# Linear attention and two gated layers on one Trainium2 core: a planner with other step lengths, a decode that moves, a q product in one piece

## The chip, the cores and the metric

The kernel runs on one core of one Trainium2 chip. The number is the device time in microseconds of one execution, the median of three; a profiled execution of the same program gives the trace. Five engines run side by side, each in its own order: TensorE (PE, matmuls, with PEld for its weight loads), VectorE (DVE), ScalarE (ACT), GpSimd (POOL), and SyncE (SP), whose queue issues the transfers (DMA).

## The reference

```python
kv  = einsum('bhsd,bhse->bhde', k, v)            # 8 batches, 8 heads, 576 tokens, 64 columns
out = einsum('bhsd,bhde->bhse', q, kv)
x   = out / sqrt(mean(out*out, -1) + 1e-6) * g_norm     # then 4608 tokens x 512
x   = (sigmoid(x @ w_gate) * (x @ w_val)) @ w_out       # 512 -> 1536 -> 512
h   = x @ w_in                                          # 512 -> 2048
y   = where(h > 0, h, exp(min(h, 0)) - 1) @ w_out2      # 2048 -> 512
```

## The kernel before

The 4608 tokens are cut in 12 blocks of 384, and two blocks make a group, six groups in all. Each fp32 factor is split in a high and a low part, so that a product is three passes over TensorE (`matmul3`, lines 384 to 386; 714 to 716 in the second layer's output).

**First layer.** For each group: attention of the next group's blocks, `in1` (the two input products and their gate), `out1` (the output product). Group 0 computes `in1` plainly. Groups 1 to 5 use a Strassen-like form (`quad`): seven products of six matmuls each instead of eight, four PSUM banks, and five additions on DVE (`plus`, line 538) that read a bank and free it. TensorE's next use of a bank waits for that addition. A group has 12 quads in `in1`, 60 additions. **Second layer.** All groups pass through `in2` (eight quads, 40 additions, and an ELU of two ACT steps and one DVE step, line 653) and `out2`, in which each product needs a split of its stationary factor: `split` (high part on ACT, line 605, low part on DVE, line 607) into one of three buffers J.

**Attention** of a block: k'v of each batch (lines 410 and 412), its copy to `kvb` (414), two q products (442) that each fill two PSUM banks for two pairs of heads, squares on ACT (449), sums on DVE (450), 13 small operations on 128x24 numbers (lines 458 to 465) that form the reciprocal root, four products with it on DVE (477), four transposes (487). The q product takes the two heads of a pair as two matmuls on 64 rows each.

**Decode.** The weights come as raw 64-bit words. `decode` makes fp32 words of them (273, 275, 277, 281), splits them (294, 296) into a buffer S and stores them; `sums` adds the Strassen sums (POOL 321 to 324, ACT 326, DVE 329). The second layer's 16 decodes (eight of `w_in`, "I", eight of `w_out2`, "O") are placed in `out1` of groups 1 to 4, four in each. The S buffers, five of them, also take the weights that are streamed for the products.

**Order.** Nothing is ordered by hand but TensorE's own list. The class `Plan` simulates all engines with a length for each step, a delay for each hand-over and a due time, and writes the instructions of each engine in the order that comes out. The chip then runs each engine's list in that order. DVE, between a wait and the next, does what the list says, late or not.

Of the kernel before, what the change touches and what calls it, by code (L numbers as in the profile page):

```python
# [21 lines left out]
P = 128  # L22
# [15 lines left out]
T_ACT, T_DVE, T_POOL = 0.53, 0.57, 1.15  # L38
# [21 lines left out]
class Plan:  # L60


    LAT = {"PE": 0.25, "DVE": 0.1, "ACT": 0.1, "POOL": 0.12, "SP": 3.5}
# [54 lines left out]
    def round(self):  # L118
# [32 lines left out]

        def begin(t, at):
# [7 lines left out]
            push(at + t.dur, "end", t)  # L160
# [4 lines left out]
        while events:  # L165
            at = events[0][0]
            while events and events[0][0] <= at + 1e-9:
# [6 lines left out]
                elif what == "free":  # L174
                    free[t.cls].append(t.slot)
                    used[t.kind] -= 1
                else:
                    idle[t.eng] = True
                    for b in t.bufs:
# [27 lines left out]
def tile_kernel(ctx: ExitStack, tc: tile.TileContext, kv, kvtail, qt, g2, w1, w2, out):  # L207
# [17 lines left out]
    kvb = [fixed([P, NP, D], F32, f"kvb{i}") for i in range(2)]  # L225
# [17 lines left out]
    plan.caps.update({"h": 32, "tmp": 11, "xf": 8, "ev": 8, "q": 4, "dec": 4, "dec2": 2, "wh": 2, "wp": 2})  # L243
# [19 lines left out]
    def decode(layer, fp, after=None):  # L263
# [3 lines left out]
        wh, wp = plan.buf("wk", "wh"), plan.buf("wk", "wp")  # L267
        word = []
        for n, f in enumerate(order):
# [3 lines left out]
            a = add("ACT", 0.65, lambda raw=raw, n=n: nc.scalar.activation(  # L273
                wh.slot[:, n, :], raw.slot[:, :, 1].bitcast(F32), AF.Copy, scale=2.0 ** -112), [ld], [raw, wh])
            b = add("ACT", 0.65, lambda raw=raw, n=n: nc.scalar.activation(
                wp.slot[:, n, :].bitcast(I32), raw.slot[:, :, 0].bitcast(U32), AF.Copy, scale=0.93 * 2.0 ** -29), [ld], [raw, wp])
            c = add("DVE", 0.8, lambda raw=raw, n=n: nc.vector.scalar_tensor_tensor(
# [3 lines left out]
        w = add("DVE", 1.3, lambda: nc.vector.scalar_tensor_tensor(  # L281
            wh.slot.bitcast(I32), wh.slot.bitcast(I32), 3, wp.slot.bitcast(I32),
            op0=ALU.logical_shift_left, op1=ALU.bitwise_or), word, [wh, wp])
        sa = plan.buf("S", "dec" if layer in "gvo" else "dec2")
        if layer == "O":
            x_hi, x_lo = (lambda: sa.slot[:, :, 0, :].rearrange("q (h n) c -> q h n c", n=2)), (lambda: sa.slot[:, :, 1, :].rearrange("q (h n) c -> q h n c", n=2))
            src_w = lambda: wh.slot.rearrange("q n (h c) -> q h n c", h=2)
        elif layer == "o":
# [5 lines left out]
        h = add("ACT", 1.05, lambda: nc.scalar.activation(x_hi(), src_w(), AF.Copy), [w, last_hi[0]], [wh, sa])  # L294
        last_hi[0] = h
        l = add("DVE", 1.3, lambda: nc.vector.tensor_tensor(x_lo(), src_w(), x_hi().bitcast(F32), op=ALU.subtract), [h], [wh, sa])  # L296
# [5 lines left out]
        if layer == "O":  # L302
            written[layer, fp] = [dma(P * 8192, lambda: nc.sync.dma_start(out=wo2[:, 0:4, fp], in_=sa.slot.bitcast(F32)), [h, l], [sa])]
            return sa, [h, l]
        d = (ws2 if layer == "I" else ws1["gv".index(layer)])[fp]
        st_a = dma(P * 6144, lambda: nc.sync.dma_start(out=d[:, 0:3], in_=sa.slot[:, 1:4].bitcast(F32)), [h, l], [sa])
        written[layer, fp] = [st_a]
        if layer == "I":
            written[layer, fp].append(sums(layer, fp, wh, w)[2])
        else:  # L310
            written["f", layer, fp] = [dma(P * 4096, lambda: nc.sync.dma_start(out=wf1["gv".index(layer)][fp], in_=wh.slot), [w], [wh])]
        return sa, [h, l]

    def sums(layer, fp, wh, w):


        d = wo2[:, 1:, fp] if layer == "O" else (ws2 if layer == "I" else ws1["gv".index(layer)])[fp]
        sf, sb_ = plan.buf("wk", "wp"), plan.buf("S", "dec2" if layer in "IO" else "st")
        A = lambda i: wh.slot[:, i // 2, i % 2 * 256:i % 2 * 256 + 256]
        T = lambda i: sf.slot[:, i // 2, i % 2 * 256:i % 2 * 256 + 256]  # L320
        s1 = add("POOL", 0.8, lambda: nc.gpsimd.tensor_tensor(T(0), A(0), A(1), op=ALU.add), [w], [wh, sf])
        s3 = add("POOL", 0.8, lambda: nc.gpsimd.tensor_tensor(T(2), A(2), A(0), op=ALU.subtract), [w], [wh, sf])
# [4 lines left out]
        if layer in "gv":  # L327
            h2.early = 12.0
# [548 lines left out]
```

## Time and profile before

| | |
|---|---|
| median of three runs | 1703.45 us (1702.94 to 1705.19) |
| profiled execution | 1705.86 us, span 1704.1 us |
| PE busy | 1670.7 us, 98% of the span |
| DVE, ACT, POOL busy | 1126.9, 810.6, 347.1 us |

The span is from the first to the last instruction. TensorE's records overlap, since matmuls are pipelined, so that its busy share says little about its pace; the idle stretches between its records, and what ended them, say where it waited. Group 1's `in1` starts near 205 us, and the second layer near 1000 us.

### The profile page before, as it was taken

The page shows a single profiled execution, that of the slowest core. Times are in us where ns is not written, and L with a number is a line of the kernel's source. Part 1 is how long each engine was busy: PE and PEld are TensorE (multiplying, and loading weights), DVE is VectorE, ACT ScalarE, POOL GpSimd, SP SyncE. Part 2 cuts the span into 40 slices and gives each one's busy share as a digit, 9 for nine tenths or more (in the row PEclk, how much of TensorE's full clock was granted, in tenths as well). Part 3 has the DMA queues.
Part 4 walks back from the last instruction along what each step waited for, and adds up shares of the span by engine and source line. Part 5 has one row for each costly group of instructions (what it writes and reads, how often), then busy time and mean ns, then how long its engine had stood idle before and what let it go on. Part 6 is the DMA issues. An engine that isn't in the chain of part 4 may idle for free.

```text
span 1704.1 us, 29327 instructions
## 1 busy us (share of the span) xinstructions
PE 1670.7 (98%) x11079; PEld 1627.6 (96%) x11079; DVE 1126.9 (66%) x2052; ACT 810.6 (48%) x1631; POOL 347.1 (20%) x326
## 2 busy tenths in 40 slices
PE   8899999999999999999999999999999999999998
PEld 6899989999899999999999998899999999999998
DVE  5768466844674385459344577768778678678675
ACT  4556324532352253236322465456566566456554
POOL 0001344502240150115022000041040140230330
PEclk9999999999999999999999999999999999999999
DMA  8988888797778787777877499888878778778774
GB/s 307 329 309 304 313 292 296 280 342 280 271 287 292 252 328 287 249 269 277 282 250 285 152 327 364 296 306 299 263 264 298 247 281 288 244 281 296 245 275 161
DMA packets 117310, 480.07 MB, mean 282 GB/s; under 512 B 11440, under 2 KB 37552, under 8 KB 87984
## 3 DMA queue, kind: packets, MB, share of 16 engines
q1 hardware_dynamic: 117168, 478.20, 78.6%
q8 instruction: 87, 1.43, 0.3%
q14 instruction: 55, 0.45, 0.1%
HBM read 393.22 MB, written 84.93 MB: 281 GB/s over the span
## 4 chain that ended last, share of the span: by engine, by line
PE 89%; DVE 7%; issue 2%; DMA 1%; ACT 0%; SPq 0%; DVEq 0%; ACTq 0%
PE psi L384 20%; PE psi L385 19%; PE psi L386 19%; PE psi L716 4%; PE psi L715 4%; PE psi L714 4%; PE psa L385 3%; PE psa L386 3%; PE psa L384 3%; PE psa L442 2%; PE psa L716 2%; PE psa L715 2%; PE psa L714 2%; DVE v L538 1%; PE psa L410 1%
## 5 line engine op out<-in xcount | busy, mean ns | idle before, releaser
L538 DVE TENSOR_TENSOR v<-v,psi 128x384 f32<-128x384 f32 x540 | 297.8, 551 | 278.3 <-PE psi L386 265.6
L384 PE MATMUL psi<-x,S 128*128 128x384 f32 x1056 | 361.0, 342 | 6.7 <-DVE v L538 6.4
L386 PE MATMUL psi<-x,S 128*128 128x384 f32 x1056 | 355.6, 337 | 4.1 <-DVE S L296 4.1
L385 PE MATMUL psi<-x,S 128*128 128x384 f32 x1056 | 355.2, 336 | 0.9 <-DVE x L495 0.9
L607 DVE TENSOR_TENSOR J<-v,J 128x384 fp32r<-128x384 f32 x336 | 200.5, 605 | 120.9 <-ACT J L605 118.3
L605 ACT ACTIVATE J<-v 128x384 fp32r<-128x384 f32 x336 | 175.8, 524 | 217.5 <-PE psa L386 70.9
L384 PE MATMUL psi<-xt,S 128*128 128x384 f32 x648 | 220.7, 341 | 0.2
L386 PE MATMUL psi<-xt,S 128*128 128x384 f32 x648 | 217.5, 336 | 0.0
L385 PE MATMUL psi<-xt,S 128*128 128x384 f32 x648 | 217.2, 335 | 0.0
L384 PEld LDWEIGHTS psi<-x,S 128*128 128x128 f32 x1056 | 199.6, 189 | 10.7 <-DVE v L538 8.2
L386 PEld LDWEIGHTS psi<-x,S 128*128 128x128 f32 x1056 | 199.8, 189 | 4.5 <-DVE S L296 4.5
L385 PEld LDWEIGHTS psi<-x,S 128*128 128x128 f32 x1056 | 199.8, 189 | 1.8 <-DVE x L495 1.4
L574 POOL TENSOR_TENSOR v<-v,v 128x384 f32<-128x384 f32 x90 | 100.4, 1124 | 430.5 <-DVE v L538 358.3
L716 PE MATMUL psi<-S,J 128*128 128x256 f32 x560 | 159.1, 284 | 2.1 <-DVE J L607 2.1
L714 PE MATMUL psi<-S,J 128*128 128x256 f32 x560 | 158.5, 283 | 0.0
L715 PE MATMUL psi<-S,J 128*128 128x256 f32 x560 | 158.5, 283 | 0.0
L384 PEld LDWEIGHTS psi<-xt,S 128*128 128x128 f32 x648 | 122.3, 189 | 2.0 <-DVE v L538 0.8
L651 ACT ACTIVATE v<-v 128x384 f32<-128x384 f32 x144 | 75.2, 523 | 101.3 <-DVE v L538 101.2
L385 PEld LDWEIGHTS psi<-xt,S 128*128 128x128 f32 x648 | 122.2, 189 | 0.0
L386 PEld LDWEIGHTS psi<-xt,S 128*128 128x128 f32 x648 | 122.1, 188 | 0.0
L542 ACT ACTIVATE v<-psi 128x384 f32<-128x384 f32 x108 | 53.1, 491 | 120.9 <-PE psi L386 119.6
L716 PEld LDWEIGHTS psi<-S,J 128*128 128x128 f32 x560 | 107.4, 192 | 3.1 <-DVE J L607 3.1
(146 smaller groups left out, 3407.0 us busy)
## 6 DMA issues: line engine op xcount, KB each, us to landing
S<-wsO SPq DMA_DIRECT2D x78, 1024.0 KB, 6.3
S<-wsI SPq DMA_DIRECT2D x48, 1024.0 KB, 5.2
S<-wso SPq DMA_DIRECT2D x36, 1024.0 KB, 6.9
S<-wsI SPq DMA_DIRECT2D x48, 768.0 KB, 6.4
raw<-w SPq DMA_DIRECT2D x68, 512.0 KB, 6.4
S<-wsg SPq DMA_DIRECT2D x24, 1024.0 KB, 5.4
S<-wsv SPq DMA_DIRECT2D x24, 1024.0 KB, 5.1
S<-wsg SPq DMA_DIRECT2D x30, 768.0 KB, 6.3
```

The lines of the kernel that those rows point to most:

```text
L384: nc.tensor.matmul(acc, wh, xh, start=first, stop=False, skip_group_check=more)
L385: nc.tensor.matmul(acc, wh, xl, start=False, stop=False, skip_group_check=more)
L386: nc.tensor.matmul(acc, wl, xh, start=False, stop=last, skip_group_check=more)
L538: return add("DVE", T_DVE, lambda: nc.vector.tensor_tensor(dst.slot, a.slot, bank[k].slot[:, :BLK], op=ALU.add), after, [dst, a, bank[k]])
L542: s1 = add("ACT", T_ACT, lambda: nc.scalar.activation(t1.slot, bank["a"].slot[:, :BLK], AF.Copy), [p1], [t1, bank["a"]])
L574: t = add("POOL", T_POOL, lambda r=r, b=b: nc.gpsimd.tensor_tensor(r.slot, r.slot, b.slot, op=ALU.mult), [d, s], [r, b])
L605: hi = add("ACT", T_ACT, lambda: nc.scalar.activation(j.slot[:, 0, :], f.slot, AF.Copy), [d], [j, f])
L607: lo = add("DVE", 0.5, lambda: nc.vector.tensor_tensor(j.slot[:, 1, :], f.slot, j.slot[:, 0, :].bitcast(F32), op=ALU.subtract), [hi], [j, f])
L651: a1 = add("ACT", T_ACT, lambda e=e, b=b: nc.scalar.activation(e.slot, ps_or_v(b), AF.Relu, scale=-1.0), [d], [e, b])
L714: nc.tensor.matmul(acc, x[0], w[:, 0], start=st, stop=False, skip_group_check=True)
L715: nc.tensor.matmul(acc, x[0], w[:, 1], start=False, stop=False, skip_group_check=True)
L716: nc.tensor.matmul(acc, x[1], w[:, 0], start=False, stop=last and f == n - 1, skip_group_check=True)
```

## The change

It has three parts. The planner gets other lengths for its steps, and a rule that lengthens a DVE and a POOL step that run at one time without PSUM. The second layer's decode works in place in the word buffers (`wk`) instead of S, stores high and low parts apart, and its 16 instances are spread over groups 1 to 5 (3, 3, 3, 3, 4). The q product takes a pair of heads as one matmul of 128 rows and 128 columns, with the pair's two k'v matrices on the diagonal of a zeroed 128x128 block of `kvb`; each PSUM bank then holds one pair, and a transpose waits for one normalising product instead of two. In the profile of the changed kernel 538 becomes 577, 607 becomes 646, 653 becomes 692, 518 becomes 557, 477 becomes 516, 442 becomes 481, 329 becomes 370.

```diff
-T_ACT, T_DVE, T_POOL = 0.53, 0.57, 1.15
+T_ACT, T_DVE, T_POOL = 0.43, 0.48, 1.0
...
-    LAT = {"PE": 0.25, "DVE": 0.1, "ACT": 0.1, "POOL": 0.12, "SP": 3.5}
+    LAT = {"PE": 0.25, "DVE": 0.13, "ACT": 0.14, "POOL": 0.14, "SP": 3.5}
...
-            end = max(t.started + t.dur for t in order)
+            end = max(t.started + t.dur for t in order if t.eng == "PE")
...
-            push(at + t.dur, "end", t)
+            stop[t] = at + t.dur
+            if t.eng in port and not any(b.cls.startswith("ps") for b in t.bufs):
+                o = port["POOL" if t.eng == "DVE" else "DVE"]
+                if o is not None and stop[o] > at:
+                    d, p = (t, o) if t.eng == "DVE" else (o, t)
+                    both = min(2 * (stop[d] - at), stop[p] - at)
+                    stop[d] += both / 2
+                    stop[p] += 0.3 * both
+                port[t.eng] = t
+            push(stop[t], "end", t)
...
-    kvb = [fixed([P, NP, D], F32, f"kvb{i}") for i in range(2)]
+    kvb = [fixed([P, NP, P], F32, f"kvb{i}") for i in range(2)]
...
-    plan.caps.update({"h": 32, "tmp": 11, "xf": 8, "ev": 8, "q": 4, "dec": 4, "dec2": 2, "wh": 2, "wp": 2})
+    plan.caps.update({"h": 32, "tmp": 11, "xf": 8, "ev": 8, "q": 4, "dec": 4, "wh": 2, "wp": 2, "wh2": 2, "wp2": 1, "sf": 1})
...
+        k = "2" if layer in "IO" else ""
+        wh, wp = plan.buf("wk", "wh" + k), plan.buf("wk", "wp" + k)
         word = []
         for n, f in enumerate(order):
...
+            a = add("ACT", 0.57, lambda raw=raw, n=n: nc.scalar.activation(
...
+        if layer in "IO":
+            d = ws2[fp] if layer == "I" else wo2[:, :, fp]
+            if layer == "I":
+                sf = plan.buf("wk", "sf")
+                A = lambda i: wh.slot[:, i // 2, i % 2 * 256:i % 2 * 256 + 256]
+                T = lambda i: sf.slot[:, i // 2, i % 2 * 256:i % 2 * 256 + 256]
+                s1 = add("POOL", 0.72, lambda: nc.gpsimd.tensor_tensor(T(0), A(0), A(1), op=ALU.add), [w], [wh, sf])
+                s3 = add("POOL", 0.72, lambda: nc.gpsimd.tensor_tensor(T(2), A(2), A(0), op=ALU.subtract), [w], [wh, sf])
+                s2 = add("POOL", 0.72, lambda: nc.gpsimd.tensor_tensor(T(1), T(0), A(2), op=ALU.subtract), [s1], [wh, sf])
+                s4 = add("POOL", 0.72, lambda: nc.gpsimd.tensor_tensor(T(3), A(3), T(1), op=ALU.subtract), [s2], [wh, sf])
+
+            def part(src, after, n0, n1):
+                out = []
+                h = add("ACT", 0.96, lambda: nc.scalar.activation(wp.slot.bitcast(F32R), src.slot, AF.Copy), after, [src, wp])
+                l = add("DVE", 1.14, lambda: nc.vector.tensor_tensor(src.slot.bitcast(F32R), src.slot, wp.slot, op=ALU.subtract), [h], [src, wp])
+                if layer == "I":
+                    view = lambda b: b.slot.rearrange("q f (k n) -> q (f k) n", k=2)[:, 4 - (n1 - n0):]
+                    to = lambda t: d[:, n0:n1, t]
+                else:
+                    view = lambda b: b.slot.rearrange("q n (h c) -> q h n c", h=2)
+                    to = lambda t: d[:, 0:4, t].rearrange("q (h n) c -> q h n c", n=2)
+                for t, b, x in ((0, wp, h), (1, src, l)):
+                    if layer == "I":
+                        out.append(dma(P * 1024 * (n1 - n0), lambda t=t, b=b: nc.sync.dma_start(out=to(t), in_=view(b)), [x], [b]))
+                    else:
+                        for k in range(2):
+                            out.append(dma(P * 2048, lambda t=t, b=b, k=k: nc.sync.dma_start(out=to(t)[:, k], in_=view(b)[:, k]), [x], [b]))
+                return out, l
+
+            st, l = part(wh, [w] + ([s3, s4] if layer == "I" else []), *((0, 3) if layer == "I" else (0, 4)))
+            written[layer, fp] = st
+            if layer == "I":
+                written[layer, fp] = st + part(sf, st[:1] + [l, s3, s4], 3, 7)[0]
+            return
...
-        if layer == "O":
-            written[layer, fp] = [dma(P * 8192, lambda: nc.sync.dma_start(out=wo2[:, 0:4, fp], in_=sa.slot.bitcast(F32)), [h, l], [sa])]
-            return sa, [h, l]
...
-                            for h in range(2):
-                                r, n = slice(h * D, h * D + D), (k * TPB + i) * D
-                                nc.tensor.matmul(o[h].slot[lo - t0:hi - t0, n:n + D], qs[k].slot[r, lo - j * BLK:hi - j * BLK],
-                                                 kvb[b % 2][r, 2 * pp + k, :], start=True, stop=True)
-            m = add("PE", 1.1, mm, lds + sum((kvdone[b, p] for b in bs for p in (2 * pp, 2 * pp + 1)), []), qs + o, queue=queue)
+                            nc.tensor.matmul(o[k].slot[lo - t0:hi - t0, i * P:i * P + P], qs[k].slot[:, lo - j * BLK:hi - j * BLK],
+                                             kvb[b % 2][:, 2 * pp + k, :], start=True, stop=True)
+            m = add("PE", 0.9, mm, lds + sum((kvdone[b, p] for b in bs for p in (2 * pp, 2 * pp + 1)), []), qs + o, queue=queue)
...
-                    x.slot.rearrange("q k (i n) -> q (k i) n", n=P)[:, :, h * D:h * D + D], o.slot[:, :BLK].rearrange("q (n d) -> q n d", d=D),
+                    x.slot[:, h, :].rearrange("q (n d) -> q n d", d=D), o.slot[:, :BLK].rearrange("q (n d) -> q n d", d=D),
...
-            x, n = xn[p // 2], [norm[p // 2, 0], norm[p // 2, 1]]
+            x, n = xn[p // 2], [norm[p // 2, p % 2]]
...
+    for t in kvb:
+        nc.vector.memset(t, 0.0)
+
+    warm = plan.slots["v"][-1].bitcast(BF16)[:, :512]
     nc.vector.memset(warm, 0.0)
...
-            for k in range(4):
-                if w2_pairs:
-                    decode(*w2_pairs.pop(0), after=plan.pe[n + (len(plan.pe) - n) * k // 12 - 40])
+            m = 4 if g == NG - 1 else 3
+            a, b = n if g == 1 else start + 30, len(plan.pe) - 20
+            for k in range(m):
+                decode(*w2_pairs.pop(0), after=plan.pe[a + (b - a) * k // m])
```

TensorE's own order stays as it was but for the q products' number of matmuls. The other engines' orders change throughout; three places on DVE follow. The names are buffers: `v`, `xp` and `sm` are work buffers, `psi` and `psa` PSUM banks, `S` streamed weights, `J`, `x` and `xt` split factors.

DVE in `in1` of group 1, at the 19th to 21st addition of the group (v<-v,psi), where the 13 small operations of a block run. Before:

```order
L538 TENSOR_TENSOR v_101<-v_93,psi_150 128x384
L464 TENSOR_TENSOR sm_147<-sm_147 128x24
L538 TENSOR_TENSOR v_93<-v_93,psi_152 128x384
L465 SCALAR_TENSOR_TENSOR sm_147<-sm_147 128x24
L463 TENSOR_TENSOR sm_147<-sm_147 128x24
L464 TENSOR_TENSOR sm_147<-sm_147 128x24
L329 TENSOR_TENSOR S_128<-wk_140,S_128 128x4x256
L465 SCALAR_TENSOR_TENSOR sm_147<-sm_147 128x24
L538 TENSOR_TENSOR v_109<-v_114,psi_151 128x384
L477 TENSOR_TENSOR xp_76<-psa_153,sm_147 128x6x64
L477 TENSOR_TENSOR xp_76<-psa_154,sm_147 128x6x64
L477 TENSOR_TENSOR xp_77<-psa_155,sm_147 128x6x64
L477 TENSOR_TENSOR xp_77<-psa_156,sm_147 128x6x64
```

and in the change, from the 18th addition on:

```order
L577 TENSOR_TENSOR v_80<-v_80,psi_152 128x384
L504 SCALAR_TENSOR_TENSOR sm_147<-sm_147 128x24
L502 TENSOR_TENSOR sm_147<-sm_147 128x24
L611 TENSOR_TENSOR v_113<-v_113,psi_151 128x384
L503 TENSOR_TENSOR sm_147<-sm_147 128x24
L504 SCALAR_TENSOR_TENSOR sm_147<-sm_147 128x24
L577 TENSOR_TENSOR v_100<-v_83,psi_150 128x384
L516 TENSOR_TENSOR xp_76<-psa_153,sm_147 128x384
L516 TENSOR_TENSOR xp_76<-psa_155,sm_147 128x384
L516 TENSOR_TENSOR xp_77<-psa_154,sm_147 128x384
L516 TENSOR_TENSOR xp_77<-psa_156,sm_147 128x384
L577 TENSOR_TENSOR v_83<-v_83,psi_152 128x384
L370 TENSOR_TENSOR S_128<-wk_141,S_128 128x4x256
```

The last small operations and the four normalising products (xp<-psa,sm) stand one addition or two earlier, and the weights' low part (S<-wk,S) behind them instead of between them.

DVE after the last addition of group 1's `in1`, where `out1` begins, whose products wait for J. Before:

```order
L538 TENSOR_TENSOR v_125<-v_125,psi_152 128x384
L518 TENSOR_TENSOR xt_73<-v_106,xt_73 128x384
L518 TENSOR_TENSOR x_70<-v_93,x_70 128x384
L518 TENSOR_TENSOR x_70<-v_118,x_70 128x384
L518 TENSOR_TENSOR xt_74<-v_80,xt_74 128x384
L518 TENSOR_TENSOR xt_74<-v_114,xt_74 128x384
L518 TENSOR_TENSOR x_71<-v_90,x_71 128x384
L518 TENSOR_TENSOR x_71<-v_95,x_71 128x384
L518 TENSOR_TENSOR x_72<-v_81,x_72 128x384
L607 TENSOR_TENSOR J_133<-v_124,J_133 128x384
L518 TENSOR_TENSOR x_72<-v_104,x_72 128x384
```

and in the change:

```order
L577 TENSOR_TENSOR v_89<-v_89,psi_152 128x384
L557 TENSOR_TENSOR xt_73<-v_95,xt_73 128x384
L557 TENSOR_TENSOR xt_73<-v_106,xt_73 128x384
L646 TENSOR_TENSOR J_133<-v_125,J_133 128x384
L557 TENSOR_TENSOR x_70<-v_100,x_70 128x384
L557 TENSOR_TENSOR x_70<-v_117,x_70 128x384
L646 TENSOR_TENSOR J_134<-v_92,J_134 128x384
L557 TENSOR_TENSOR xt_74<-v_80,xt_74 128x384
L557 TENSOR_TENSOR xt_74<-v_114,xt_74 128x384
L557 TENSOR_TENSOR x_71<-v_90,x_71 128x384
L646 TENSOR_TENSOR J_135<-v_113,J_135 128x384
```

Before, eight splits of the next group's factor (x and xt) stand ahead of the fourth J of `out1`; now two stand ahead of it, and two more ahead of the fifth.

DVE where group 1's `in2` ends and its `out2` begins (the same in groups 2 to 5). Before:

```order
L538 TENSOR_TENSOR v_103<-v_103,psi_151 128x384
L653 SCALAR_TENSOR_TENSOR v_105<-v_105,v_97 128x384
L607 TENSOR_TENSOR J_135<-v_91,J_135 128x384
L607 TENSOR_TENSOR J_133<-v_127,J_133 128x384
L653 SCALAR_TENSOR_TENSOR v_119<-v_119,v_103 128x384
L607 TENSOR_TENSOR J_134<-v_81,J_134 128x384
L607 TENSOR_TENSOR J_135<-v_94,J_135 128x384
L607 TENSOR_TENSOR J_133<-v_112,J_133 128x384
```

and in the change:

```order
L577 TENSOR_TENSOR v_91<-v_91,psi_151 128x384
L692 SCALAR_TENSOR_TENSOR v_103<-v_103,v_90 128x384
L646 TENSOR_TENSOR J_135<-v_112,J_135 128x384
L692 SCALAR_TENSOR_TENSOR v_120<-v_120,v_91 128x384
L646 TENSOR_TENSOR J_133<-v_98,J_133 128x384
L646 TENSOR_TENSOR J_134<-v_116,J_134 128x384
L646 TENSOR_TENSOR J_135<-v_96,J_135 128x384
L646 TENSOR_TENSOR J_133<-v_94,J_133 128x384
```

The last ELU step (v<-v,v) moves ahead of the second of the J shown.

## Rows read from the trace of the kernel before

**Rows 1.** The page's chain that ended last, by engine.
```profile
PE 89%; DVE 7%; issue 2%; DMA 1%; ACT 0%; SPq 0%; DVEq 0%; ACTq 0%
```
**Rows 2.** Busy time by stage, with instructions, granted clock (PEclk) and DMA share.
```profile
core 0: us, PE busy (x) PEld busy (x) DVE busy (x) ACT busy (x) POOL busy (x), PEclk, DMA share, GB/s
...
205.00:325.00 120.00, 114.92 (x781) 110.03 (x779) 81.22 (x144) 54.20 (x102) 61.83 (x64) 0.99 0.81 290
...
810.00:1000.00 190.00, 190.00 (x1098) 190.00 (x1098) 88.05 (x164) 59.34 (x120) 18.41 (x18) 1.00 0.70 251
1000.00:1704.00 704.00, 697.57 (x4704) 685.09 (x4702) 530.23 (x983) 397.67 (x833) 134.12 (x120) 1.00 0.79 277
```
**Rows 3.** TensorE's waits, 100 to 810 us: for whom, total, times, longest.
```profile
PE psi L384 <- DVE v L538: 6.4, 4, 3.2
PE psi L385 <- DVE J L607: 4.7, 5, 1.5
PE psa L487 <- DVE xp L477: 3.3, 2, 2.6
```
**Rows 4.** TensorE's waits over the whole span, other lines of that view.
```profile
PE psi L386 <- DVE S L296: 4.1, 1, 4.1
PE psa L410 <- DMA kv<-kv: 3.8, 2, 2.3
...
PE psi L716 <- DVE J L607: 2.1, 5, 0.4
```
**Rows 5.** DVE in order of time, 236 to 262 us: start, duration, instruction.
```profile
243.26 0.17 DVE L463 TENSOR_TENSOR sm<-sm 128x24 f32<-128x24 f32 x1
...
247.17 1.05 DVE L465 SCALAR_TENSOR_TENSOR sm<-sm 128x24 f32<-128x24 f32 x1
...
249.81 1.81 DVE L329 TENSOR_TENSOR S<-wk,S 128x1024 fp32r<-128x1024 f32 x1
...
252.64 1.94 DVE L477 TENSOR_TENSOR xp<-psa,sm 128x384 f32<-128x384 f32 x4
254.50 1.20 DVE L538 TENSOR_TENSOR v<-v,psi 128x384 f32<-128x384 f32 x2
```
**Rows 6.** TensorE in order of time behind that: idle time and its releaser in brackets.
```profile
255.09 0.59 PE L384 MATMUL psi<-x,S 128*128 128x384 f32 x1 [3.23 <-DVE v L538]
```
**Rows 7.** Busy time by stretch, two short ones; the columns of rows 2.
```profile
251.00:260.00 9.00, 5.77 (x25) 5.42 (x25) 6.10 (x12) 3.06 (x5) 4.78 (x6) 0.81 0.48 175
...
455.00:468.00 13.00, 10.27 (x52) 9.60 (x51) 11.48 (x22) 6.71 (x12) 6.26 (x6) 0.87 0.85 288
```
**Rows 8.** DVE in order of time where group 1's out1 has begun.
```profile
319.36 2.64 DVE L518 TENSOR_TENSOR x<-v,x 128x384 fp32r<-128x384 f32 x2
...
325.09 0.55 DVE L607 TENSOR_TENSOR J<-v,J 128x384 fp32r<-128x384 f32 x1
```
**Rows 9.** TensorE in order of time at four places: transposes, k'v, q products.
```profile
58.39 0.33 PE L385 MATMUL psi<-x,S 128*128 128x384 f32 x1
58.56 0.34 PE L386 MATMUL psi<-x,S 128*128 128x384 f32 x1
58.74 1.47 PE L487 MATMUL psa<-ident,xp 128*128 128x128 f32 x12
59.97 0.42 PE L384 MATMUL psi<-x,S 128*128 128x384 f32 x1
...
109.07 0.69 PE L410 MATMUL psa<-kv 128*64 128x64 f32 x16
...
109.95 0.44 PE L384 MATMUL psi<-x,S 128*128 128x384 f32 x1
...
125.87 1.56 PE L442 MATMUL psa<-kvb,v 64*128 64x64 f32 x24
127.36 0.45 PE L384 MATMUL psi<-x,S 128*128 128x384 f32 x1
...
231.05 1.88 PE psa L442 x32
```
**Rows 10.** DVE, then TensorE, in order of time where group 1's out2 begins.
```profile
1160.93 0.55 DVE L653 SCALAR_TENSOR_TENSOR v<-v,v 128x384 f32<-128x384 f32 x1
...
1162.54 2.69 DVE L607 TENSOR_TENSOR J<-v,J 128x384 fp32r<-128x384 f32 x2
1165.15 1.37 DVE L653 SCALAR_TENSOR_TENSOR v<-v,v 128x384 f32<-128x384 f32 x1
...
1165.38 0.29 PE L716 MATMUL psi<-S,J 128*128 128x256 f32 x1
...
1167.05 0.39 PE L716 MATMUL psi<-S,J 128*128 128x256 f32 x1 [0.42 <-DVE J L607]
```
**Rows 11.** ACT's waits over the whole span, one line of that view.
```profile
ACT S L294 <- DMA wsI<-S: 4.8, 4, 2.1
```

More of the change, by code (lines that the diff above doesn't have):

```diff
@@ L150, in can @@
                 used.get(c, 0) + k <= self.caps.get(c, 999) for c, k in kinds.items())
+        port = {"DVE": None, "POOL": None}
+        stop = {}
         def begin(t, at):
@@ L293, in decode @@
             src_w = lambda: wh.slot.rearrange("q f (k n) -> q (f k) n", k=2)
-        h = add("ACT", 1.05, lambda: nc.scalar.activation(x_hi(), src_w(), AF.Copy), [w, last_hi[0]], [wh, sa])
+        h = add("ACT", 0.96, lambda: nc.scalar.activation(x_hi(), src_w(), AF.Copy), [w, last_hi[0]], [wh, sa])
         last_hi[0] = h
-        l = add("DVE", 1.3, lambda: nc.vector.tensor_tensor(x_lo(), src_w(), x_hi().bitcast(F32), op=ALU.subtract), [h], [wh, sa])
+        l = add("DVE", 1.14, lambda: nc.vector.tensor_tensor(x_lo(), src_w(), x_hi().bitcast(F32), op=ALU.subtract), [h], [wh, sa])
         if layer == "o":
@@ L325, in sums @@
+        s2 = add("POOL", 0.72, lambda: nc.gpsimd.tensor_tensor(T(1), T(0), A(2), op=ALU.subtract), [s1], [wh, sf])
+        s4 = add("POOL", 0.72, lambda: nc.gpsimd.tensor_tensor(T(3), A(3), T(1), op=ALU.subtract), [s2], [wh, sf])
         sfv = lambda: sf.slot.rearrange("q f (k n) -> q (f k) n", k=2)
-        h2 = add("ACT", 1.05, lambda: nc.scalar.activation(sb_.slot[:, :, 0, :], sfv(), AF.Copy), [s3, s4], [sf, sb_])
-        if layer in "gv":
-            h2.early = 12.0
-        l2 = add("DVE", 1.3, lambda: nc.vector.tensor_tensor(
+        h2 = add("ACT", 0.96, lambda: nc.scalar.activation(sb_.slot[:, :, 0, :], sfv(), AF.Copy), [s3, s4], [sf, sb_])
@@ L330, in sums @@
+        h2.early = 12.0
+        l2 = add("DVE", 1.14, lambda: nc.vector.tensor_tensor(
             sb_.slot[:, :, 1, :], sfv(), sb_.slot[:, :, 0, :].bitcast(F32), op=ALU.subtract), [h2], [sf, sb_])
@@ L412, in mm @@
                             nc.tensor.matmul(pb.slot[e, :D], tl.slot[r, p // 2, 0, e], tl.slot[r, p // 2, 1, e], start=False, stop=True)
-            m = add("PE", 0.9, mm, [ld, ld_t], [t, tl, pb], queue=queue)
-            kvdone[b, p] = [add("ACT", 0.25, lambda pb=pb, p=p: nc.scalar.activation(
-                kvb[b % 2][:, p, :], pb.slot[:, :D], AF.Copy), [m] + kvread.get((b - 2, p), []), [pb])]
+            m = add("PE", 0.98, mm, [ld, ld_t], [t, tl, pb], queue=queue)
+            kvdone[b, p] = [add("ACT", 0.2, lambda pb=pb, p=p, e=slice(h * D, h * D + D): nc.scalar.activation(
+                kvb[b % 2][e, p, e], pb.slot[e, :D], AF.Copy), [m] + kvread.get((b - 2, p), []), [pb]) for h in range(2)]
     def attention(j, queue, direct=None, bank="psa", gap=3, hold=None):
@@ L468, in attention @@
         for part in ([ops] if hold is not None else [[op] for op in ops]):
-            last = [add("DVE", 0.2 * len(part), lambda part=part: [op() for op in part], last, [sm])]
+            last = [add("DVE", 0.1 if len(part) == 1 else 0.22 * len(part), lambda part=part: [op() for op in part], last, [sm])]
         res = []
```

47 lines of the change are left out of this document (20 added, 27 removed).

## The prediction

> **What bounds the kernel now.** I read the chain that ended last first: 89% of it lies on TensorE and 7% on DVE [rows 1]. So the time is TensorE's work plus what TensorE waits, and an edit counts only if it shortens that work or one of those waits. The busy time by stage shows where the waits are [rows 2]: from 810 to 1000 us TensorE is idle nowhere and the clock is full; from 1000 to 1704 us it is busy 697.57 of 704, which bears no large gain; in group 1's `in1` (205 to 325 us) it is busy 114.92 of 120. The list of its waits gives the sum: between 100 and 810 us it waits for DVE alone, for additions (6.4 us in four), for J (4.7 in five) and for the normalised attention output (3.3 in two), 14.4 us in all [rows 3]. The other waits are 4.1 us for DVE in the prologue, 3.8 for the first K and V, and five of 0.4 us at the starts of `out2` in groups 1 to 5 [rows 4].
>
> DVE in time order shows how such a wait arises. Near 243 us a small operation takes 0.17 us, near 247 the same kind takes 1.05; a weights' low part of 1.81 us follows, then four normalising products, 1.94 together, and only then the addition that TensorE needs [rows 5]. TensorE stood 3.23 us [rows 6], and the clock, granted in full before, averages 0.81 from 251 to 260 us and 0.87 from 455 to 468, where TensorE had waited 2.6 us for a transpose's input [rows 7]. With levels of 2.4 and 1.2 GHz that loses 0.19 x 9 and 0.13 x 13, 1.7 us each time, an estimate that assumes TensorE would have worked throughout. At 319 us two of the next group's splits take 2.64 us between them, and the J that `out1` waits for ends only at 325.64 [rows 8]. In each case DVE is not short of time over the stage (81 of 120 us); it does the late thing first. What can be had is therefore 14.4 + 3.4, about 18 us.
>
> **The change, part by part.** *New order of DVE.* The excerpts show the three causes moved. At the 19th to 21st addition the small operations and the normalising products stand one or two additions earlier, and the low part that stood ahead of them behind. At `out1` the fourth J has two splits ahead of it in place of eight; a split takes 1.3 us [rows 8] so six of them are 7.9 us of DVE's time moved behind J, more than any wait there (1.5 at the longest, [rows 3]). In groups 2 to 4 the decode no longer fills `out1` alone, so the pieces that stood between additions there are fewer. I do not take all 18 us: a quad's 42 passes at the pace of 0.17 a pass (58.39 to 58.56, [rows 9]) take TensorE some 7.3 us, and the durations of before, added up over the new order, still give DVE 8.4 in one quad of group 1 (9.0 at worst in the old order; many rows, too many to show). For what stays I write 4.3 us, an estimate, part by part: 0.7 near 252, 0.8 near 459, 0.8 near 623 and 778 together, 1.0 in group 0's plain phase, 1.0 new in that quad of 8.4. Bounds for what stays are 0.8 (only the plain phase) and 18 (the waits come back elsewhere). Sum: -13.7 us.
>
> *The q product in one piece.* A warm step of before runs from 125.87 to the next product at 127.36: 1.49 us for 24 passes of 64 columns on 64 rows; the step of 32 passes took 1.88 [rows 9]. There are 14 of the first outside the prologue and 6 of the second. The new step has half as many passes, of 128 columns on 128 rows. No row of before has these. The nearest on the whole array are the transposes: 12 passes of 128 columns in 1.23 us (58.74 to 59.97), so 0.1025 each, 12 of them 1.23 and 16 of them 1.64. That gives 14 x 0.26 + 6 x 0.24, about -5 us. The lower bound is by k'v, whose 20 passes of 64 columns on 128 rows took 0.88 us (109.07 to 109.95): 0.088 for 128 columns, 1.06 and 1.41 us per step, -8.8 us in all. The upper bound is by q's own pace: two 64-row passes side by side took 0.124 us for 64 columns, and if 128 columns on the whole array go at that pace, a step takes 2.98 or 3.76 us, and the sum is +32. I take the transposes, since they have the same shape and type and stand in the same stage.
>
> The rows leave the question of side-by-side running open, and a page speaks against the edit: the Trainium skill, "TensorEngine Tiling (Array Packing)", section "Theoretical Speedup", gives up to a factor of 2 for splitting the array when a dimension is 64 or less, so that giving the split up would double the step. No run here has both forms; the transposes' 0.1025 us a pass does not bear it out.
>
> *Where `out2` begins.* Here the order costs. Before, two J took 2.69 us, until 1165.23, and TensorE's first pass with the low part of the second of them started at 1165.38; an ELU step of 1.37 followed, and then the third J, for which TensorE waited 0.42 [rows 10]. Now the ELU step stands ahead of the second J, which then ends near 1166.6; its pass waits some 1.2 us, and the third J, no later than before, is no longer waited for. That is 0.8 more in each of five groups, +4; where DVE is quick (the same ELU step took 0.55 near 1161 [rows 10]) it would be nothing. I take +0.6 each, nearer to the slow row, since POOL works there in all five groups: +3.0 us, bounds 0 and +4.
>
> *The rest at nothing.* Clearing `kvb` lies under the wait for the first K and V, of 2.3 us at the longest [rows 4]; uncovered it would cost its own duration, of the order of two splits, 2.6 us, once. The 32 more copies on ACT, a few us in all, lie in ACT's idle half (54.20 busy of 120, [rows 2]). The decode's stores come in more and smaller pieces, two or four for one, but TensorE waits for no weight transfer after the prologue [rows 3, 4], with the DMA engines at 0.70 to 0.81 [rows 2]; and the five S buffers, free of the decode, serve streaming alone. The decode keeps its work on POOL and DVE, and where it now lies in `in1` it adds to those quads: that is the 1.0 new above. The wait in the prologue stays as it is, since DVE's order there is the same: 0, plus or minus 1.
>
> The sum is -13.7 - 5.0 + 3.0 = -15.7 us, from the profiled 1705.9 to 1690.2. That execution is 2.4 above the median of three, so I forecast **1688**.
>
> **The rivals.** What this kernel's measurement can tell from no change is about 0.2%, 3.4 us: 1700.0 to 1706.9 counts as the same.
>
> *More than that.* If nearly all of the waits go (17.2 of 18), q runs at the k'v pace (-8.8) and `out2` loses nothing, the sum is -26: 1677. For it speak the lone causes above; against it the 8.4-us quad.
>
> *The waits move.* The new order is again made without the chip. The operations that were slow were slow in some places only (0.17 against 1.05 for one kind [rows 5]), and an order that does not know of these will stall in others. Then only q and `out2` count: -2.0, 1701.5. Against it: the causes in the excerpts are plain mis-orderings by several operations, not by fractions of one.
>
> *q doubles.* The upper bound above: -13.7 + 32 + 3.0 = +21, 1725, slower. It ties when the 20 steps grow by 10.7 us together, 0.54 each (a first step of 2.03 us), and is slower by over 0.2% from 0.71 each. Against it stand the transposes.
>
> *ACT is caught behind a store.* The `w_in` decode now has one buffer for its high part, so its second copy on ACT waits for the landing of the first one's store, and ACT's later work (TensorE's gate and ELU, the high part of J) is queued behind it. Before, the like wait for such a store was 2.1 us at the longest [rows 11]. Eight such waits, all passed on to TensorE, are 17 us: -15.7 + 17, about 1705. It ties when each passes on 2.0 us and is slower by over 0.2% from 2.4 each. Against it: the four waits of before, 4.8 us, appear nowhere in TensorE's list [rows 3, 4].
>
> **How the numbers follow.** Chances: the forecast 0.56, more than that 0.17, the waits move 0.15, q doubles 0.05, ACT caught 0.07. The forecast's own range is 1681 (q by k'v, -3.8; `out2` free, -3) to 1695 (twice as much waiting stays, +4.3; `out2` at its bound, +1; the prologue, +1). The range for all is 1675 to 1704: it leaves out q doubling, more than half of ACT caught and the tail below 1675, under 0.2 together. Faster by over 0.2% holds the forecast, the larger gain, and about a quarter of the moved waits: 0.78. The same: the rest of these and half of ACT caught, 0.12. Slower: q doubling, the other half, and a little of the moved waits, 0.10.
>
> **What the profile after would show.** Waits of TensorE for DVE between 100 and 810 us of 3 to 6 us in place of 14.4, none over 1.5, and a granted clock of 1.00 through 251 to 260 and 455 to 468; a q step of about 1.23 us with 12 passes (1.06: the k'v pace; near 3: doubled); five waits of about 1.0 us in place of 0.4 where `out2` begins; 810 to 1000 us as full as before; the prologue's 4.1 us unchanged. I would be wrong if the list holds 14 us again under other tiles, if a weight transfer stands among TensorE's releasers, if ACT's wait for a store reaches TensorE's list, or if the step at one of the small operations grows because POOL now works in `in1`.

## The result, and the profile after

The changed kernel takes 1685.67 us (median of four, 1684.35 to 1688.01), the kernel before 1703.66 on the same chip: a ratio of 0.9895, 95% interval 0.9878 to 0.9912, which is 17.9 us less. The profiled execution takes 1685.98 us, its span is 1684.2. The forecast was 1688.

The chain that ended last, by engine, which answers to [rows 1]:
```profile
PE 95%; DVE 2%; DMA 1%; issue 1%; ACT 0%; SPq 0%; DVEq 0%
```
DVE's share falls from 7% to 2%. Busy time by stage in the changed kernel, in the columns of [rows 2]; the two short stretches are those of [rows 7]:
```profile
205.00:325.00 120.00, 119.62 (x768) 116.02 (x767) 81.28 (x149) 51.74 (x100) 59.84 (x62) 1.00 0.83 299
251.00:260.00 9.00, 9.00 (x56) 8.94 (x55) 5.31 (x9) 3.44 (x6) 7.03 (x8) 1.00 0.95 342
455.00:468.00 13.00, 13.00 (x78) 12.97 (x77) 12.88 (x18) 9.98 (x22) 13.00 (x13) 1.00 0.82 310
810.00:1000.00 190.00, 189.65 (x1094) 189.33 (x1093) 114.71 (x209) 82.26 (x164) 25.44 (x26) 1.00 0.85 304
```
From 205 to 325 us DVE is busy for as long as before, 81.3 us, and yet TensorE is idle 0.4 us there instead of 5.1; the clock stays full. All of TensorE's waits in the changed kernel from 100 to 810 us (first line), then its three largest waits for DVE over the whole span (for whom, total, times, longest):
```profile
PE psi L425 <- DVE v L577: 1.2, 3, 0.5
...
PE psi L755 <- DVE J L646: 5.1, 5, 1.0
PE psi L425 <- DVE v L577: 4.2, 5, 2.6
PE psi L427 <- DVE S L344: 4.1, 1, 4.1
```
The 14.4 us of [rows 3] (14.6 with one wait of 0.2 that these rows leave out) are 1.2 now. The five waits at the starts of `out2` have grown from 0.4 to 1.0 us each, and there is a wait of 2.6 us that was not there. TensorE in order of time at the q products and at these two waits:
```profile
126.64 0.33 PE L427 MATMUL psi<-x,S 128*128 128x384 f32 x1
126.81 1.50 PE L481 MATMUL psa<-kvb,v 128*128 128x128 f32 x12
128.07 0.42 PE L425 MATMUL psi<-x,S 128*128 128x384 f32 x1
...
231.59 2.18 PE L481 MATMUL psa<-kvb,v 128*128 128x128 f32 x16
233.53 0.42 PE L425 MATMUL psi<-xt,S 128*128 128x384 f32 x1
...
1081.48 0.34 PE L427 MATMUL psi<-x,S 128*128 128x384 f32 x1
...
1084.38 0.44 PE L425 MATMUL psi<-x,S 128*128 128x384 f32 x1 [2.56 <-DVE v L577]
...
1143.28 0.38 PE L755 MATMUL psi<-S,J 128*128 128x256 f32 x1 [1.02 <-DVE J L646]
```
The step of 12 passes takes 1.26 us for 1.49 before, that of 16 takes 1.94 for 1.88 [rows 9]. DVE at the second and third of these places in the changed kernel:
```profile
1081.49 0.69 DVE L651 COPY xp<-psa 128x512 f32<-128x512 f32 x1 [4.57 <-DMA out<-xp]
1082.10 0.68 DVE L394 TENSOR_TENSOR kv<-wk,kv 128x512 fp32r<-128x512 f32 x1
1082.69 0.55 DVE L577 TENSOR_TENSOR v<-v,psi 128x384 f32<-128x384 f32 x1
...
1139.26 1.39 DVE L646 TENSOR_TENSOR J<-v,J 128x384 fp32r<-128x384 f32 x1
1140.57 1.37 DVE L692 SCALAR_TENSOR_TENSOR v<-v,v 128x384 f32<-128x384 f32 x1
1141.87 2.29 DVE L646 TENSOR_TENSOR J<-v,J 128x384 fp32r<-128x384 f32 x3
```
Near 1081 us, where group 0's second layer ends, DVE stands 4.57 us in front of an output copy into `xp`, because an earlier store from `xp` has not landed, and the addition that frees TensorE's bank is queued behind the copy. Near 1140 the ELU step stands ahead of the J that TensorE waits for.

### The profile page after: what moved, and what is told of

It reads as the page before. It is cut to its first block, busy times and chain, and to the rows that moved or that the text cites. A ratio compares the mean times of both kernels' runs of the same rounds, so it can differ in the third digit from the quotient of the medians.

```text
span 1684.2 us, 28777 instructions
## 1 busy us (share of the span) xinstructions
PE 1657.7 (98%) x10759; PEld 1622.3 (96%) x10759; DVE 1106.6 (66%) x2054; ACT 813.4 (48%) x1663; POOL 334.4 (20%) x326
## 4 chain that ended last, share of the span: by engine, by line
PE 95%; DVE 2%; DMA 1%; issue 1%; ACT 0%; SPq 0%; DVEq 0%
PE psi L425 21%; PE psi L426 21%; PE psi L427 21%; PE psi L755 4%; PE psi L753 4%; PE psi L754 4%; PE psa L426 4%; PE psa L427 4%; PE psa L425 4%; PE psa L481 2%; PE psa L754 2%; PE psa L753 2%; PE psa L755 2%; PE psa L451 1%; PE psa L526 1%
## 5 line engine op out<-in xcount | busy, mean ns | idle before, releaser
L646 DVE TENSOR_TENSOR J<-v,J 128x384 fp32r<-128x384 f32 x336 | 205.0, 617 | 126.0 <-ACT J L644 125.0
L692 DVE SCALAR_TENSOR_TENSOR v<-v,v 128x384 f32<-128x384 f32 x144 | 87.8, 610 | 58.8 <-ACT v L691 58.8
```

The source lines that it names most:

```text
L646: lo = add("DVE", T_DVE, lambda: nc.vector.tensor_tensor(j.slot[:, 1, :], f.slot, j.slot[:, 0, :].bitcast(F32), op=ALU.subtract), [hi], [j ...
L692: res[int(n[0]) - 1, int(n[1]) - 1] = (e, add("DVE", T_DVE, lambda e=e, b=b: nc.vector.scalar_tensor_tensor(e.slot, e.slot, -1.0, ps_or_v( ...
```

## The experiments

Each ran beside the kernel before; ratios are to it, in brackets the 95% interval, and 0.001 is 1.7 us. Its median was 1704.61 in the first four runs, 1706.49 in the next four and 1704.90 in the last four, so ratios are compared, not medians.

**One part at a time.** The first run has only the q product's part of the diff:
```diff
...
-                            for h in range(2):
...
+                            nc.tensor.matmul(o[k].slot[lo - t0:hi - t0, i * P:i * P + P], qs[k].slot[:, lo - j * BLK:hi - j * BLK],
+                                             kvb[b % 2][:, 2 * pp + k, :], start=True, stop=True)
...
```


> The kernel before with the q products on the whole array alone (and a transpose that waits for one normalising product). Theory (the gain is the order of DVE, about 14 us, and TensorE's shorter q steps, about 5): 4 to 6 us under the kernel before, near 1698.5, with DVE's waits in group 0's and group 1's stages of the same size as before. Rival (the q products bring most, since four transposes wait for less): 10 us or more under it.

1699.74 us, 0.9969 (0.9959 to 0.9979): 5.3 us. TensorE's waits for DVE from 100 to 810 us are 15.8 us, no fewer than before. So q is worth about what TensorE's steps save, and no more.

The second has only the planner's part:
```diff
-T_ACT, T_DVE, T_POOL = 0.53, 0.57, 1.15
+T_ACT, T_DVE, T_POOL = 0.43, 0.48, 1.0
...
+                    stop[d] += both / 2
+                    stop[p] += 0.3 * both
...
```


> The kernel before with the planner's new lengths and collision rule alone; q and decode as before. Theory: the new order removes most of the waits by itself, 8 to 14 us under the kernel before (1690 to 1696), with five waits near 1.0 us at the starts of out2 in place of 0.4. Rival (the decode's new place removes them): within 4 us of the kernel before, with TensorE's waits for DVE between 100 and 810 us still over 10 us.

1707.73 us, 1.0015 (1.0006 to 1.0024): 2.6 us slower, the rival's time but not the rival's waits. TensorE's waits in it, 100 to 810 us:
```profile
PE psi L400 <- DVE v L554: 6.7, 10, 2.5
PE psi L400 <- DMA S<-wsv: 6.1, 2, 3.1
```
The waits for J and for the normalised output are gone, 8.0 us of them in [rows 3], but those for additions are 6.7 us, and TensorE now waits 6.1 us for streamed weights, at 619 and 779 us; the five waits at `out2` are 1.0 us each. Of the wait of 3.2 us near 255 us 0.6 is left.

The third has only the decode's part:
```diff
-        sa = plan.buf("S", "dec" if layer in "gvo" else "dec2")
...
+            m = 4 if g == NG - 1 else 3
+            a, b = n if g == 1 else start + 30, len(plan.pe) - 20
...
```


> The kernel before with the new decode alone (in place, over five groups); the planner's numbers and q as before. Theory: it takes away only the waits beside the decode in out1, 2 to 6 us under the kernel before, and the two long waits in group 1 (3.2) and group 2 (2.6) stay. Rival (the decode's place is the cause): 10 us or more under it.

1692.72 us, 0.9933 (0.9921 to 0.9945): 11.4 us, the rival's number. Its waits, 100 to 810 us:
```profile
PE psi L409 <- DVE v L563: 3.2, 1, 3.2
PE psi L410 <- DVE J L632: 2.0, 2, 1.1
PE psa L512 <- DVE xp L502: 0.7, 1, 0.7
...
```
Of the two long waits only the one near 255 us (3.2) is left. That near 462 us is gone, as it was with the planner's part alone; in the run in place alone, below, 1.9 us of it stay, near 456 us. So each new plan moves this wait, and no run shows what it hangs on.

The fourth is the changed kernel without the planner's part, the second's diff taken back.


> The changed kernel with the planner's old lengths and without the collision rule; q and decode as changed. Theory: 7 to 11 us over the changed kernel (1693 to 1697), as it keeps only q and the decode's part, and the waits at the starts of out2 fall back to 0.4 us. Rival (the numbers matter little): within 3 us of the changed kernel.

1685.20 us, 0.9884 (0.9869 to 0.9899): as fast as the changed kernel. All of TensorE's waits behind 100 us in it:
```profile
PE psi L739 <- DVE J L630: 2.1, 5, 0.4
PE psi L410 <- DVE J L630: 2.0, 2, 1.0
PE psi L409 <- DVE v L561: 2.0, 3, 1.0
PE psi L409 <- ACT v L565: 1.6, 1, 1.6
PE psa L510 <- DVE xp L500: 1.1, 1, 1.1
```
They are 8.8 us, as against 9.3 in the changed kernel, in other places. So decode and q make the gain without the planner's part: 11.4 and 5.3 us alone, 19.8 together by the ratios.

That the planner's part alone is worth nothing is true of the sum and not of its stages. TensorE's order is the same in all runs, so one and the same pass can be looked up in each. This is a transpose near the end of group 3's `in1`, in the kernel before, with the planner's part, with the decode's part, and in the changed kernel:
```profile
627.41 0.49 PE L487 MATMUL psa<-ident,xp 128*128 128x128 f32 x3
615.97 0.49 PE L503 MATMUL psa<-ident,xp 128*128 128x128 f32 x3
618.40 0.49 PE L512 MATMUL psa<-ident,xp 128*128 128x128 f32 x3
606.50 0.49 PE L526 MATMUL psa<-ident,xp 128*128 128x128 f32 x3
```
The planner's part alone is 11.4 us ahead there, the decode's part alone 9.0. Near 800 us the first has given back all but 1.6, at the two waits for weights and at additions near 626 and 785 us (1.0 and 2.5), in the stages where the decode stands as it did before; the second is some 13 ahead.

**What it is in the decode.** The decode's part has two halves. First its new places, still through S, in the kernel before:
```diff
-            for k in range(4):
-                if w2_pairs:
-                    decode(*w2_pairs.pop(0), after=plan.pe[n + (len(plan.pe) - n) * k // 12 - 40])
+            m = 4 if g == NG - 1 else 3
+            a, b = n if g == 1 else start + 30, len(plan.pe) - 20
+            for k in range(m):
+                decode(*w2_pairs.pop(0), after=plan.pe[a + (b - a) * k // m])
```


> The kernel before with the decode's new places alone (3, 3, 3, 3, 4 over groups 1 to 5, through in1 and out1), still through the S buffers; q and the planner's numbers as before. Theory one (the waits came from the decode standing densely ahead of the additions and J): most of the 11.9 us that the whole new decode gave, 8 to 12 us under the kernel before. Theory two (they came from the S buffers that the decode held): within 4 us of the kernel before, or slower, since S is held for longer in in1.

1694.16 us, 0.9938 (0.9924 to 0.9952): 10.6 us. Then in place, in the old places but for group 1, where the four are spread evenly over `out1`:
```diff
-        sa = plan.buf("S", "dec" if layer in "gvo" else "dec2")
+        if layer in "IO":
+            d = ws2[fp] if layer == "I" else wo2[:, :, fp]
...
-                    decode(*w2_pairs.pop(0), after=plan.pe[n + (len(plan.pe) - n) * k // 12 - 40])
+                    decode(*w2_pairs.pop(0), after=plan.pe[n + (len(plan.pe) - n) * k // (4 if g == 1 else 12) - (0 if g == 1 else 40)])
```


> The kernel before with the decode in place alone (no S buffers), still four in out1 of each of the groups 1 to 4 (in group 1 evenly over out1, as the place of before has no buffers free); q and the planner's numbers as before. Theory one (density): within 4 us of the kernel before, with the waits near 623, 640, 778 and 796 us still there. Theory two (S buffers): 8 to 12 us under it.

1693.85 us, 0.9935 (0.9920 to 0.9950): 11.1 us. Each half alone gives the whole, so neither theory holds as it was put. The waits that they leave from 100 to 810 us differ: new places alone leave 2.0 us near 253 and 2.0 for J, in place alone leaves 2.0 near 255, 1.9 near 456 and 1.0 for J. The two have in common what DVE does where `in1` ends. Busy time from 602 to 658 us, where group 3's `in1` passes into `out1`, in the kernel before:
```profile
602.00:658.00 56.00, 53.26 (x308) 52.17 (x307) 52.48 (x84) 33.93 (x64) 24.09 (x22) 1.00 0.79 292
```
in the run with new places alone, which reaches that point 11 us earlier:
```profile
591.00:647.00 56.00, 56.00 (x327) 55.55 (x326) 40.54 (x77) 24.93 (x51) 15.56 (x14) 1.00 0.74 277
```
and in the run in place alone, which reaches it 8 us earlier:
```profile
594.00:650.00 56.00, 56.00 (x327) 55.35 (x326) 42.73 (x80) 28.19 (x56) 19.71 (x18) 1.00 0.79 285
```
DVE is busy 52.5 of 56 us before, and 40.5 and 42.7 in these; TensorE then waits for nothing there. The decode's own steps on DVE in these stretches take 18.4 us before (17 of them), 4.5 with new places alone (5) and 7.6 in place alone (8). So working in place thins the decode out as new places do. In place, only one high-part buffer and two word buffers are open to it; that this is why it thins out was not tested.

How this delays J can be seen near 642 us, where TensorE waited 1.4 us before for the fourth J of `out1`. DVE from the last addition of `in1` to that J, then GpSimd, before:
```profile
634.70 0.54 DVE L538 TENSOR_TENSOR v<-v,psi 128x384 f32<-128x384 f32 x1
...
637.28 2.66 DVE L518 TENSOR_TENSOR x<-v,x 128x384 fp32r<-128x384 f32 x2
...
640.88 1.07 DVE L607 TENSOR_TENSOR J<-v,J 128x384 fp32r<-128x384 f32 x1
...
639.49 1.05 POOL L323 TENSOR_TENSOR wk<-wk,wk 128x256 f32<-128x256 f32 x1
```
and with new places alone:
```profile
624.39 0.54 DVE L538 TENSOR_TENSOR v<-v,psi 128x384 f32<-128x384 f32 x1
...
626.98 1.84 DVE L518 TENSOR_TENSOR xt<-v,xt 128x384 fp32r<-128x384 f32 x2
...
629.21 0.55 DVE L607 TENSOR_TENSOR J<-v,J 128x384 fp32r<-128x384 f32 x1
...
626.60 1.33 POOL L516 TENSOR_TENSOR v<-v,v 128x384 f32<-128x384 f32 x1
```
DVE is not late when this begins: the last addition starts 0.70 us behind TensorE's first pass of `out1` before, and 1.16 behind it here. Five splits stand between it and J in both. From the start of the addition to the end of J it is 7.25 us before and 5.37 here. GpSimd works beside DVE until 641.5 us before, with four of the decode's Strassen sums (such as L323) among its work from 631 us on, and until 627.9 here, with none. That its work is what makes DVE's steps long fits the counts at the end of this text; no run moved the sums by themselves.

A third way to thin it, one number in the kernel before:
```diff
-                    decode(*w2_pairs.pop(0), after=plan.pe[n + (len(plan.pe) - n) * k // 12 - 40])
+                    decode(*w2_pairs.pop(0), after=plan.pe[n + (len(plan.pe) - n) * k // 12])
```


> The kernel before with one number changed: the decode's four pieces of work are released 40 of TensorE's steps later, so that none stands between the last additions of in1; still four in out1 of groups 1 to 4, still through S. Theory (DVE came late to the additions and J because decode pieces stood between the last additions of in1): the waits near 306, 324, 623, 640, 778 and 796 us go, 7 to 11 us under the kernel before. Rival (it is the amount of decode in out1, or the S buffers it holds): within 4 us of the kernel before, with waits in out1 or for weights in their place.

1697.56 us, 0.9950 (0.9935 to 0.9966): 8.5 us. The six waits named went, 7.6 us of [rows 3], and a new one took part of their place:
```profile
686.26 0.42 PE L384 MATMUL psi<-xt,S 128*128 128x384 f32 x1 [4.16 <-DMA S<-wsv]
```
So it is the decode pieces among `in1`'s last additions that brought these waits, as the theory has it. The run moves the pieces on DVE and those on GpSimd together and does not part them. The 8.5 us hide more: the pass that starts at 644.04 us before starts at 629.01 here, 15.0 us earlier, and 5.5 of these are lost around the new wait, behind which the granted clock is 0.88 from 686 to 700 us. I take it that the pieces, pushed later and still through S, hold buffers that the next group's weights need; this was not tested. The runs with places in both stages, or with no use of S, have no wait for weights from 100 to 810 us.

**The planner's rule.** The changed kernel with the new lengths but without the rule for DVE and GpSimd:
```diff
...
-                    stop[d] += both / 2
-                    stop[p] += 0.3 * both
...
```


> The changed kernel with the new step lengths but without the rule that lengthens a DVE and a GpSimd step that run together. Theory (the waits went with the decode's place, not with the planner's numbers): within 3 us of the changed kernel. Rival (the rule is what keeps DVE in time): 5 us or more over it, with waits for DVE in group 1's and group 2's in1 again.

1694.18 us, 0.9931 (0.9917 to 0.9945): 6 us over the changed kernel by the ratios, against my expectation of 3 at most. The largest of TensorE's waits behind 100 us, and the five at `out2`:
```profile
PE psi L409 <- DVE v L561: 6.9, 10, 2.7
...
PE psi L739 <- DVE J L630: 1.0, 5, 0.2
```
The old, longer lengths without the rule do as well as the shorter ones with it. The new length of a DVE step is 0.48 us, and beside GpSimd such a step took up to 1.40 in the changed kernel; I take it that without the rule the plan counts on a DVE that is faster than the chip's.

**The two new waits.** The changed kernel with the last ELU step of each `in2` held back:
```diff
...
-                e.slot, e.slot, -1.0, ps_or_v(b), op0=ALU.add, op1=ALU.max), [a2], [e, b], due=1.0))
+            last = fp == NF2 // 2 - 1 and n == "21"
...
+                e.slot, e.slot, -1.0, ps_or_v(b), op0=ALU.add, op1=ALU.max), [a2], [e, b], due=6.0 if last else 1.0)
+            t.early = 1.0 if last else None
...
```


> The changed kernel with the last ELU step of each in2 held back behind three J. Theory (each of the five waits of 1.0 us is that step, ahead of the second J): the five waits fall to 0 to 0.4 us, 3 to 6 us under the changed kernel. Rival (DVE is short of time there whatever the order): the waits move to the next J, within 2 us of the changed kernel.

1679.36 us, 0.9860 (0.9841 to 0.9879), span 1677.9, 6.3 under the changed kernel's. All five waits are gone (and the one near 1081 us is 1.5). DVE there:
```profile
1138.33 3.98 DVE L646 TENSOR_TENSOR J<-v,J 128x384 fp32r<-128x384 f32 x3
1142.22 0.54 DVE L693 SCALAR_TENSOR_TENSOR v<-v,v 128x384 f32<-128x384 f32 x1
```
The ELU step, 1.37 us in its old place, takes 0.54 here, because GpSimd has finished by then.

The changed kernel with two output copies in a word buffer:
```diff
-                        e = plan.buf("xp")
+                        e = plan.buf("xp" if blk == 0 or i == 0 else "wk")
```


> The changed kernel with two of the six output copies at the end of group 0's second layer written into a word buffer in place of xp. Theory (the wait of 2.6 us near 1081 us is DVE's copy, which waits for an earlier store from xp to land, with an addition queued behind it): that wait goes, 2 to 3 us under the changed kernel. Rival (the addition is late for another reason): no change, the wait at the same place.

1682.80 us, 0.9873 (0.9857 to 0.9888), span 1681.1, 3.1 under the changed kernel's; the wait of 2.6 us is gone. Both together:


> The changed kernel with both mends, the ELU step behind three J and the two output copies in a word buffer. Theory (two separate waits): both gains add, 8 to 10 us under the changed kernel (1676 to 1678), and TensorE's waits behind 100 us come to under 3 us. Rival (one hides the other): no better than the first mend alone.

1677.88 us, 0.9837 (0.9823 to 0.9850), span 1675.5: 27.8 us under the kernel before and 9.9 under the changed one by the ratios; the fastest of all. All that TensorE waits behind 100 us in it:
```profile
PE psi L425 <- DVE v L577: 1.6, 4, 0.5
```

**A miss.** To see whether GpSimd is what slows DVE near 1140 us, its combinations were held back in the changed kernel:
```diff
-                        [da, db] + used.get(d, []) + ([] if dst else [gate]), [d, a, b])
+                        [da, db] + used.get(d, []) + hold + ([] if dst else [gate]), [d, a, b])
...
+        p1 = product("a", 2, B11, True, True)
+        hold = [plan.pe[2 - n]]
         T1 = combine(B12, B11)
...
-        p1 = product("a", 2, B11, True, True)
```


> The changed kernel with GpSimd's combinations in out2 held back until the third product of out2 is done, so that GpSimd is idle while the ELU step and the first J are formed. Theory (the ELU step and the J there take 1.3 us each only because GpSimd works beside them): they take 0.55 us, the five waits of 1.0 us go, 4 to 6 us under the changed kernel. Rival (they are slow for another reason): they take 1.3 us still, and the time is the changed kernel's or worse.

1704.09 us, 0.9995 (0.9986 to 1.0005), 17 us over the changed kernel by the ratios. The hold ended at the wrong point: GpSimd was set free just as these J came up, with most of its combinations still to do. DVE, then GpSimd, there:
```profile
1140.61 5.21 DVE L646 TENSOR_TENSOR J<-v,J 128x384 fp32r<-128x384 f32 x4
1145.75 7.80 DVE L646 TENSOR_TENSOR J<-raw,J 128x384 fp32r<-128x384 f32 x6
...
1161.63 0.56 DVE L646 TENSOR_TENSOR J<-wk,J 128x384 fp32r<-128x384 f32 x1 [0.27 <-ACT J L644]
...
1138.93 7.76 POOL L728 TENSOR_TENSOR wk<-v,raw 128x384 f32<-128x384 f32 x6
...
1149.23 10.31 POOL L728 TENSOR_TENSOR v<-v,v 128x384 f32<-128x384 f32 x8
```
The test that was meant, a place without GpSimd, did not come about, but its opposite did. GpSimd works from 1138 to 1159.5 us, and J after J takes 1.3 us; behind that a J takes 0.56, as those of 1144.85 and 1145.98 us do in the changed kernel, where GpSimd is done by 1143. TensorE's products there follow each other at 1.29 us in place of 1.08, which is most of the 17 us.

## Why the prediction was right, and where its reasons were not

**The q product: right in sum.** -5.0 was predicted; the run with it alone gives -5.3. The step of 12 passes is the transposes' 1.23 within 0.03. That of 16 was mis-sized, 1.94 for 1.64: it has pieces of 64 tokens, which the transposes have not, and I take that to be the difference. What makes up for it is an edge that I left out: the last pass ahead of the step starts 0.17 us before it, and did 0.27 before it in the old form. Fourteen steps at 0.23 + 0.10 + 0.02 (the next pass) and six at 0.06 are 5.3. The doubling did not come. That rule of the Trainium skill, "TensorEngine Tiling (Array Packing)", section "Theoretical Speedup", is not borne out by this step: 12 whole passes take 1.26 us, 24 split ones took 1.49.

**Where `out2` begins: right.** Five waits of about 1.0 were predicted and are there; +3.0 us (0.6 each) is what they cost, and the mend that moves the ELU step takes them away.

**DVE's waits: the size nearly, the cause in part.** -13.7 was predicted; what the profiled time leaves is -19.9 + 5.3 - 3.0 = -17.6. The list was to hold 3 to 6 us from 100 to 810 us and holds 1.2. These waits fell by 13.4 and the clock in the two stretches of [rows 7] came back to 1.00, an estimated 3.4, against which stand 2.6 new near 1081. Of the rest, 3.4, half lies ahead of 59 us: the transposes that start at 58.74 us before [rows 9] start at 57.04 in the changed kernel. Most of the other half is what eight waits fewer give beyond their idle time, an estimate from 0.16 each (last section).

The step that is true only in part is "New order of DVE". It read the whole gain off the excerpts, as J that stands behind two splits instead of eight, and normalising products that stand earlier. For the two long waits, near 255 and 462 us, this can stand: with the planner's part alone, the decode left as it was, they are 0.6 and nothing. For the six waits where `in1` ends, 7.6 us, it is not needed. The run with new places alone has five splits between the last addition and the fourth J of group 3, as the kernel before has, and no wait there. What counted was the sentence I gave least room, that the decode's pieces between the additions become fewer; the run with one number changed takes these six waits away. A split's 1.3 us, too, is its time beside GpSimd; with GpSimd idle it takes 0.55, as the one at 641.87 us before, so that the 7.9 us for six of them are the most that they can be. With either part alone TensorE is 9 to 11 us ahead at 627 us, so two causes were at work where I reckoned with one, and that the size came out near is partly luck. The statement that DVE "is not short of time over the stage" holds for group 1's 120 us and was wrong for the 56 us around the end of group 3's `in1`, where it was busy 52.5. I had not looked at that stretch by itself.

**The planner's part: nothing net, as a sum.** Beside the new decode and q it takes away waits of 2.0 us for J, 1.6 for ACT and 1.1 for the normalised output, and gives back 3.0 at `out2` and 2.2 at additions. Alone it gains 11.4 us by 627 us, loses them to late weights and additions, and ends 2.6 us slower; without its rule the changed kernel is 6 us slower.

**What was not foreseen.** "810 to 1000 us as full as before" nearly holds (189.65 of 190). The wait near 1081 us is a DVE copy behind a store that had not landed. In the trace before, the same copy stood 2.4 us without harm; I had not followed that idle time into the new order. The prologue's 4.1 us stayed, as predicted, and no wait for ACT stands in TensorE's list.

## What to carry to other kernels

Before reading an order for what stands ahead of what, measure how full the engine is over the few tens of microseconds ahead of each wait: in the kernel before, DVE is busy 62.7 of 120 us from 508 to 628 us (52%), and 52.5 of 56 (94%) where that stage passes into the next. There each of three ways to thin it helped. Test the parts of a change apart even when the sum comes out as forecast, and look up one and the same pass of TensorE in each run: a part that sums to nothing may have gained and lost 11 us. After a gain, list the remaining waits once more: two places, of one line each, were worth 9.9 us, over half of what the change gave.

## What the runs showed of the hardware

Counted over the changed kernel's trace by how much of a DVE step lies beside a GpSimd step: J's low parts (both inputs in SBUF) take 0.56 us with no GpSimd step beside them (407 of them) and 1.03 on average, 1.40 at most, with over 90% beside GpSimd (28); the additions, with one input in PSUM, take 0.55 in both cases (359 and 164). The Trainium skill, "SBUF — State Buffer", section "Who interferes with whom", says that a DVE instruction with two SBUF inputs contends with a GpSimd instruction that reads SBUF. The trace agrees: 0.56 against 1.03 with two such inputs, 0.55 against 0.55 with one. In the miss above, where GpSimd's work was bunched beside them, 92 of J's low parts lie so and take 1.26 on average, and the 347 with none beside them 0.56.

In both places looked at, a wait cost TensorE 0.16 or 0.17 us more than its idle time: from 1081.48 to 1084.38 us are 2.90, less one pass of 0.17 is 2.73, for an idle time of 2.56; from 1141.98 to 1143.28 are 1.30, less one pass of 0.12 is 1.18, for 1.02.
